# Attention, routed attention and a gated MLP on one core: the product with V on 128 partitions throughout, and a new issue order

## The chip, the cores and the metric

One core of a Trainium2 chip runs the whole program. The metric is the device time of one execution in microseconds (us); the median of several is given. The core has TensorE (PE: matmuls and transposes; PEld its weight loads), VectorE (DVE), ScalarE (ACT), GpSimd (POOL) and SyncE (SP, which here issues DMAs). Each engine works through its own queue in order; semaphores make one wait for another.

## What is computed

Three stages, each taking the output of the one before, over batch 8, sequence 576:

```python
# 1: attention, 8 heads of 64, block-causal in blocks of 64 (q, k, v: 8 x 8 x 576 x 64)
scores = where(block_i >= block_j, q @ k.T / 8, -1e9)
x = softmax(scores) @ v                      # heads side by side: 8 x 576 x 512
# 2: four routed attention experts of 64, causal, each token keeps its best 2 of 4
w = softmax over the top 2 of (x @ w_gate)
out = sum over e of w[e] * (softmax(causal(x wq[e] (x wk[e]).T / 8)) @ (x wv[e]) @ wo[e])
# 3: gated MLP with a product along the sequence
u, v = split(relu(out @ w_in)); v = layernorm(v)
y = (u * (w_spatial @ v + b_spatial)) @ w_out
```

Inputs and output are 32-bit; `w_in` and `w_out` arrive 64-bit.

## The kernel before

**Numbers in two halves.** Most operands are held as two 16-bit tiles, a rounded high part and the remainder (a cast, then a subtraction). A product is three matmuls, high x high, high x low, low x high, summed in PSUM.

**Pairs.** The heads are taken two at a time: four pairs of stage 1 and two pairs of experts per batch, 48 in all, keyed (batch, 0 to 3) and (batch, 4 to 5). A pair's sequence of 576 is five chunks: four of 128 and one of 64. For the last chunk the two heads' 64 queries share one block of 128. A pair goes through these steps:
- `load_qk`, `load_v` (lines 247 to 273): DMAs into a buffer `nat`, on SP, ACT or POOL. `mags` (line 275) finds the largest magnitudes, on DVE or ACT. `prep_qk` transposes q and k on PE and splits them (lines 343, 232, 238), `prep_v` splits v.
- `scores` (from line 371), four steps `sc` with j = 0 to 3 for four groups of query chunks: matmuls into a PSUM buffer `duo` (lines 389 to 407), row maxima on DVE (410, 412), the exponent's limit on ACT or DVE (420, 422), exponentials on ACT (426, 431). For j = 0 to 2 the matmuls contract over 64 partitions, one head in each half of the array; j = 3 uses 128.
- `weights` (line 437), steps `w`: the exponentials in 32 bits (`pf`, 1024, 1024, 512 and 576 columns for j = 0 to 3) are cast to 16 bits on ACT, DVE or POOL (lines 350, 352, 354) and the remainder is taken on DVE or POOL (line 448) into `p16`. `weights_t` (line 450) sends `p16` through a DMA transpose on SP (line 453) into `pT`, keys on the partitions.
- `av` (line 455), the product with V in three parts (24, 24 and 42 matmuls on PE, line 464). Chunk 4 runs over five key blocks; the fifth holds 64 keys, and its matmuls read partitions 0 to 63 only. One column of V is ones, so the row sums come along. Columns 1088 to 1151 and 2240 to 2303 of `p16`, behind the 64 keys, are cleared once at the start, and their rows of `pT` are zero.
- `halves` (line 488), step `x`: divides, casts, takes the remainder (line 498) and transposes by DMA into `x`.

There are four `duo` buffers (two PSUM banks each), four `nat`, four `pf`, three `p16`, four `pT`.

**Startup** converts and splits the weights once, among the first batches' steps: `split` is the split of wq/wk, wv and the gate (DVE part at line 238), `win`, `hl`, `wm`, `wout` make one matrix of wo and w_in.

**The dense part of a batch** (function `dense`): projections (line 804), values of the experts (827), the gate, the two expert pairs, then the first MLP product (883), the normalisation (`norm`, 921 to 927), the gated product along the sequence (`gating2`, 978 to 986, steps `gs`) and the last product (998) with its store.

**What sets the order.** All steps are generators, listed once with `add` (line 1294) and cut in pieces, one per engine visit. The tuple `ORDER` (line 1014) names for each next piece the number of its step: the whole program is issued by walking that tuple (line 1540), which fixes the order on each engine's queue and which buffer each step gets. `WAYS` (line 1198) says for each kind of step, with one letter or two per batch, on which engine it is issued: A, D, G or S for ACT, DVE, POOL or SP; "AG" in `w` is a cast on ACT and a subtraction on POOL. The last letter stands for all later batches. The planner that wrote the two tables is not in the kernel; the piece costs in `add` calls stay in the file but set nothing.

```python
for i in ORDER:
    t = named[i]
    ...
    run(t)
```

Of the kernel before, what the change touches and what calls it, by code (L numbers as in the profile page):

```python
# [21 lines left out]
P = 128  # L22
# [10 lines left out]
def attn_moe_gmlp_kernel(  # L33
# [18 lines left out]
    B, H, S, D = q.shape  # L52
# [402 lines left out]
    def av(p, wt):  # L455
# [3 lines left out]
        def chunk(c, hh, col, nk, pT):  # L459
            o = 65 * c  # L460
            for kk in range(nk):
                r = P if kk < 4 else 64
                for i, (t, a, n) in enumerate(((0, 0, 65), (0, 66, 64), (1, 0, 65))):
                    T.matmul(ps[:, hh, o:o + n], pT[0:r, col(t, kk):col(t, kk) + P], p.v[0:r, hh, kk, a:a + n],  # L464
                             start=kk == 0 and i == 0, stop=kk == nk - 1 and i == 2)
# [299 lines left out]
    def dense(b, keep):  # L765
# [821 lines left out]
```

## Time and profile before

| | |
|---|---|
| device time, median of 3 runs | 1056.85 us (1054.46 to 1057.37) |
| the profiled execution | 1055.53 us, of which the span of its instructions is 1053.8 us |
| mean granted TensorE clock | 0.928 of full speed |
| busy in the span | PE 902.1, DVE 791.7, ACT 669.8, POOL 469.6 us |

A busy time is the time in which at least one instruction of the engine was running. Matmuls overlap one another in the array, so that PE's busy time holds pauses shorter than one matmul's own duration; what a run of matmuls costs is read from the start of its first to the start of what follows. An engine's wait is put down to what came last before it. The granted clock is the share of full speed that TensorE was given in a stretch.

### The profile page before, as it was taken

To read this page: it belongs to the slowest core of one execution; us is meant where nothing else is said; L and a number is where in the kernel's file an instruction comes from. 1 tells how busy PE (TensorE), PEld (TensorE's weight loads), DVE (VectorE), ACT (ScalarE), POOL (GpSimd) and SP (SyncE) were. 2 spreads that over 40 slices of the span, in tenths; PEclk is the share of its full clock that TensorE was granted. 3 is DMA by queue.
4 is the path that set the end of the run, shared out by engine and by line. 5 is a ranking of instruction groups with operands and counts; after the bars stand their busy time and mean duration, and the time that the engine had idled before them with its cause. 6 is when DMAs were issued, how large, how long until landed. Compare 5 with 4: busy or idle time off the path is not lost.

```text
span 1053.8 us, 25324 instructions
## 1 busy us (share of the span) xinstructions
PE 902.1 (86%) x10118; PEld 654.3 (62%) x10118; DVE 791.7 (75%) x1616; ACT 669.8 (64%) x1206; POOL 469.6 (45%) x394
## 2 busy tenths in 40 slices
PE   1576697578999889988998899999998999799988
PEld 1355575466676657666776667667765776577654
DVE  4898989879887878687866787768768786657351
ACT  1786767767666756686858667677676756537331
POOL 4287665566323506454524538443463244304210
PEclk9968798688999899998999999999999999899989
DMA  9879866699659865889758986898479546924501
GB/s 212 162 146 186 183 134 142 128 168 194 122 101 179 160 125 101 156 169 179 138 111 164 160 160 119 147 186 160 78 150 176 96 76 121 189 31 72 106 21 45
DMA packets 492390, 143.66 MB, mean 136 GB/s; under 512 B 479712, under 2 KB 485968, under 8 KB 492272
## 3 DMA queue, kind: packets, MB, share of 16 engines
q1 hardware_dynamic: 472928, 131.38, 66.2%
q0 software_dynamic: 2832, 6.73, 2.3%
q10 hardware_dynamic: 16512, 3.94, 1.9%
q8 instruction: 79, 1.29, 0.5%
q14 instruction: 39, 0.32, 0.1%
HBM read 38.19 MB, written 9.44 MB: 45 GB/s over the span
## 4 chain that ended last, share of the span: by engine, by line
PE 46%; DVE 10%; ACT 5%; issue 2%; DMA 1%; ACTq 0%; SPq 0%; POOL 0%; DVEq 0%; POOLq 0%
PE duo L978 9%; PE duo L464 8%; PE duo L998 8%; PE duo L804 5%; PE duo L883 4%; PE duo L962 3%; PE duo L389 3%; DVE st L410 3%; PE duo L827 2%; ACT pf L431 2%; PE duo L404 2%; PE duo L343 1%; DVE qk L238 1%; DVE p L448 1%; ACT vn L924 1%
## 5 line engine op out<-in xcount | busy, mean ns | idle before, releaser
L448 POOL TENSOR_TENSOR p<-pf,p 128x1024 f16<-128x1024 f32 (+2 forms) x111 | 201.1, 1818 | 172.8 <-ACT p L350 74.4
L464 PEld LDWEIGHTS <-pT 128*128 128x128 f16 (+1 forms) x4320 | 159.6, 102 | 44.6 <-issue 23.4
L410 DVE TENSOR_REDUCE st<-duo 128x2 f32<-128x1024 f32 (+2 forms) x192 | 150.3, 816 | 36.4 <-PE duo L399 22.3
L389 PE MATMUL duo<-qk 64*128 64x256 f16 (+3 forms) x1152 | 118.5, 323 | 26.5 <-ACT qk L232 11.3
L464 PE MATMUL duo<-v,pT 128*128 128x65 f16 (+3 forms) x2880 | 117.0, 200 | 16.7 <-ACT pf L431 10.6
L978 PE MATMUL duo<-wsp,vn 128*128 128x288 f16 x896 | 122.9, 291 | 8.0 <-ACT vn L924 3.6
L431 ACT ACTIVATE pf<-duo,st,es 128x512 f32<-128x512 f32 (+3 forms) x224 | 122.0, 617 | 10.4 <-DVE rr L485 3.7
L998 PE MATMUL duo<-wo,gT 128*128 128x512 f16 (+1 forms) x480 | 109.2, 384 | 2.9 <-ACT pf L431 1.9
L498 POOL TENSOR_TENSOR xh<-pf,xh 128x640 f16<-128x640 f32 x40 | 57.6, 1439 | 121.4 <-ACT xh L350 115.5
L978 PEld LDWEIGHTS <-vn 128*128 128x128 f16 x896 | 87.0, 99 | 33.8 <-ACT vn L924 4.4
L804 PE MATMUL duo<-x,wqk 128*128 128x288 f16 x768 | 98.3, 287 | 0.6 <-DVE qk L238 0.5
L448 DVE TENSOR_TENSOR p<-pf,p 128x576 f16<-128x576 f32 (+2 forms) x81 | 83.3, 1034 | 15.2 <-ACT p L350 9.2
L389 PEld LDWEIGHTS <-qk 64*128 64x128 f16 x1152 | 52.3, 99 | 60.6 <-issue 35.9
L804 PEld LDWEIGHTS <-wqk 128*128 128x128 f16 x768 | 74.3, 98 | 21.5 <-issue 1.5
L350 ACT CAST p<-pf 128x1024 f16<-128x1024 f32 (+2 forms) x104 | 82.6, 809 | 1.2 <-DMA pT<-p 0.2
L998 PEld LDWEIGHTS <-gT 128*128 128x128 f16 (+1 forms) x480 | 47.3, 101 | 56.8 <-issue 5.3
L354 POOL TENSOR_SCALAR p<-pf 128x1024 f16<-128x1024 f32 (+2 forms) x46 | 42.7, 928 | 88.8 <-ACT pf L431 47.8
L343 PE MATMUL duo<-ident,nat 128*128 128x128 f32 x320 | 58.4, 319 | 18.3 <-ACT pf L431 6.1
L420 ACT ACTIVATE st<-st,ln,es 128x2 f32<-128x2 f32 (+2 forms) x91 | 35.0, 388 | 61.5 <-DVE st L410 44.3
L431 ACT ACTIVATE pf<-duo,st,mt 128x256 f32<-128x256 f32 (+3 forms) x128 | 69.9, 616 | 5.7 <-DVE st L422 4.3
L404 PE MATMUL duo<-qk 128*128 128x288 f16 x288 | 50.5, 318 | 20.1 <-ACT pf L431 15.2
L295 DVE TENSOR_REDUCE mst<-nat 128x1 f32<-128x640 f32 (+1 forms) x54 | 60.7, 1133 | 8.9 <-DMA nat<-in_v_dram 5.8
(269 smaller groups left out, 1742.7 us busy)
## 6 DMA issues: line engine op xcount, KB each, us to landing
out_dram<-o SPq DMA_DIRECT2D x16, 512.0 KB, 3.4
nat<-in_q_dram SPq DMA_DIRECT2D x52, 128.0 KB, 2.9
nat<-in_k_dram SPq DMA_DIRECT2D x52, 128.0 KB, 2.9
nat<-in_v_dram SPq DMA_DIRECT2D x40, 128.0 KB, 2.8
wf<-in_moe_w_in_dram SPq DMA_DIRECT2D x8, 512.0 KB, 4.8
nat<-in_v_dram POOLq DMA_DIRECT2D x20, 128.0 KB, 4.1
pT<-p SPq DMA_TRANSPOSE x144, 4.8
wf<-in_moe_w_out_dram SPq DMA_DIRECT2D x4, 512.0 KB, 4.9
```

The lines of the kernel that those rows point to most:

```text
L295: V.tensor_reduce(st[:, a, o], t[:, a].rearrange("p i c d -> p i (c d)"), op=OP.max, axis=AX.X, apply_absolute_value=True)
L343: T.transpose(ps[:, P * c:P * c + r], p.nat[0:r, i, c, :], ident[0:r, 0:r])
L350: A.copy(hi, src)
L389: T.matmul(ph[:, hh, o:o + w], p.q[hs, a, ts], p.k[hs, bb, 0:w], start=i == 0, stop=False)
L404: T.matmul(ps[:, MID + a:MID + a + n], p.q[:, l, 512:640], p.k[:, r, a:a + n], start=i == 0, stop=i == 2 and not (p.moe and a))
L410: V.reduce_max(st[:, 0, 2 * c:2 * c + 2], ph[:, :, off[c]:off[c] + P * (c + 1)], axis=AX.X)
L431: A.activation(pf[:, n * hh + off[c]:n * hh + off[c] + w], ph[:, hh, off[c]:off[c] + w], AF.Exp, bias=st[:, 1, 2 * c + hh:2 * c + hh + 1], ...
L448: (V if way[1] == "D" else G).tensor_sub(lo, src, hi)
L464: T.matmul(ps[:, hh, o:o + n], pT[0:r, col(t, kk):col(t, kk) + P], p.v[0:r, hh, kk, a:a + n], start=kk == 0 and i == 0, stop=kk == nk - 1 ...
L804: T.matmul(ps[:, MID + a:MID + a + w], wqk16[:, l, c, 2 * n + i, :], x16[c][:, r, a:a + w], start=m == 0, stop=m == 11)
L978: T.matmul(ps[:, MID + a:MID + a + n], vn[:, l, ds_], wsp16[:, r, c, a:a + n], start=i == 0, stop=False)
L998: T.matmul(ps[0:r, i], gT[:, x, d, P * c:P * c + r], wo16[:, y, d, :], start=m == 0, stop=m == 11)
```

## The change

In the product with V the fifth key block is read over all 128 partitions instead of 64. The matmuls are as many as before:

```diff
         def chunk(c, hh, col, nk, pT):
             o = 65 * c
             for kk in range(nk):
-                r = P if kk < 4 else 64
                 for i, (t, a, n) in enumerate(((0, 0, 65), (0, 66, 64), (1, 0, 65))):
-                    T.matmul(ps[:, hh, o:o + n], pT[0:r, col(t, kk):col(t, kk) + P], p.v[0:r, hh, kk, a:a + n],
+                    T.matmul(ps[:, hh, o:o + n], pT[:, col(t, kk):col(t, kk) + P], p.v[:, hh, kk, a:a + n],
                              start=kk == 0 and i == 0, stop=kk == nk - 1 and i == 2)
```

The two tables are new. `ORDER` has the same 3800 entries in another sequence (62 and 63 load the first pair, 66 and 67 the second, 70 and 71 the third; 1, 2 and 17 load weights; 158 and 159 make the first pair's scales, 78 and 79 its transposes):

```diff
     ORDER = (
-        0, 62, 62, 62, 62, 62, 62, 62, 1, 1, 1, 1, 1, 1, 1, 1, 66, 1, 67, 1, 67, 1, 67, 1, 64, 1, 66, 63, 66, 66,
-        158, 63, 66, 158, 63, 158, 66, 159, 17, 66, 159, 2, 159, 70, 159, 2, 70, 159, 3, 2, 70, 2, 70, 2, 70, 70, 2,
...
+        0, 62, 62, 62, 62, 62, 62, 62, 1, 1, 1, 1, 1, 1, 66, 1, 67, 1, 67, 1, 67, 1, 64, 66, 1, 63, 66, 1, 66, 158,
+        63, 1, 66, 158, 63, 158, 66, 159, 17, 66, 159, 2, 159, 70, 71, 71, 71, 159, 2, 159, 159, 78, 70, 79, 78, 2,
...
```

`WAYS` differs in 215 of its steps' entries. Two kinds of `w` as an example (first dense pair of each batch, j = 0 and 1), and the magnitudes of the first pair:

```diff
     WAYS = {
...
-        "w.4.0": ("AG", "AD", "GG", "AG", "AG", "AG", "DD", "AG"),
+        "w.4.0": ("AG", "AG", "DD", "GG", "AD", "AG", "AD", "DD"),
...
-        "w.4.1": ("DG", "GD", "GD", "GD", "DG", "GG", "GG", "DG"),
+        "w.4.1": ("DD", "DD", "GD", "DD", "DD", "GG", "AD", "DD"),
...
-        "mg.0.1": ("D",), "mg.1.0": ("D", "D", "D", "A", "D"), "mg.1.1": ("D", "D", "D", "A", "D", "A", "D"),
+        "mg.0.0": ("D", "D", "D", "A", "D", "A", "A", "D"), "mg.0.1": ("D", "D", "D", "A", "A", "A", "D", "A"),
```

Counted over all steps, before and after (number on each engine):

| kind | ACT | DVE | POOL | SP |
|---|---|---|---|---|
| casts of `w` and `x` | 144, 123 | 44, 61 | 52, 56 | |
| subtractions of `w` and `x` | | 89, 105 | 151, 135 | |
| limits of `sc` | 151, 132 | 41, 60 | | |
| magnitudes `mg` | 10, 20 | 54, 44 | | |
| split of v `pv` | 22, 21 | 5, 5 | 5, 6 | |
| `norm`, first operation | | 12, 16 | 28, 24 | |
| `norm`, last operation | | 12, 14 | 28, 26 | |
| remainder of `gs` | | 26, 20 | 6, 12 | |
| loads `lq` (7 DMAs each) | 3, 5 | | 3, 4 | 26, 23 |
| loads `lv` (3 DMAs each) | 2, 3 | | 10, 7 | 20, 22 |

Of the subtractions of 1024 columns, DVE has 30 before and 39 after, POOL 66 and 57.

## Rows read from the trace of the kernel before

**Rows 1.** The page: its first line and part 1 (busy us, share of the span, instructions).
```profile
span 1053.8 us, 25324 instructions
PE 902.1 (86%) x10118; PEld 654.3 (62%) x10118; DVE 791.7 (75%) x1616; ACT 669.8 (64%) x1206; POOL 469.6 (45%) x394
```

**Rows 2.** Stretches: us, PE, PEld, DVE, ACT, POOL busy (instructions), PEclk, DMA share, GB/s.
```profile
0.00:52.00 52.00, 20.30 (x118) 12.66 (x118) 34.93 (x100) 21.33 (x43) 16.78 (x41) 1.00 0.90 189
52.00:263.00 211.00, 151.75 (x1759) 118.12 (x1760) 185.84 (x326) 152.41 (x270) 140.45 (x108) 0.78 0.81 160
263.00:790.00 527.00, 490.97 (x5772) 358.69 (x5770) 406.17 (x829) 360.19 (x656) 239.08 (x194) 0.97 0.76 143
790.00:1053.80 263.80, 239.04 (x2473) 164.84 (x2471) 164.75 (x363) 135.87 (x239) 73.30 (x53) 0.95 0.49 94
```

**Rows 3.** Stretches of line 464's matmuls alone: us, PE busy (instructions), PEclk, DMA share, GB/s.
```profile
0.00:263.00 263.00, 40.46 (x900) 0.82 0.82 165
263.00:1053.80 790.80, 134.31 (x3420) 0.96 0.67 127
```

**Rows 4.** Timeline of PE, two stretches: start us, us, engine, line, operation, count.
```profile
546.63 1.63 PE L464 MATMUL duo<-v,pT 128*128 128x65 f16 x48
548.10 1.24 PE L998 MATMUL duo<-wo,gT 128*128 128x512 f16 x5
...
467.44 0.35 PE L389 MATMUL duo<-qk 64*128 64x128 f16 x6
467.61 0.21 PE L399 MATMUL duo<-m_col,m_row 64*128 64x64 bf16 x2
467.75 1.76 PE L464 MATMUL duo<-v,pT 128*128 128x65 f16 x42
469.44 0.86 PE L343 MATMUL duo<-ident,nat 128*128 128x128 f32 x5
```

**Rows 5.** Stretches of 0.1 us, line 464's matmuls alone (columns as in rows 3).
```profile
390.70:390.80 0.10, 0.10 (x10) 1.00 0.00 0
391.00:391.10 0.10, 0.10 (x5) 1.00 0.53 115
```

**Rows 6.** Line 464 on PE, 390.95 to 390.97 us: count, ns min/median/max, starts, forms.
```profile
L464 PE MATMUL duo<-v,pT x4: 191/192/201, 390.8 to 391.0; 128*128 128x65 f16 x2, 128*128 128x64 f16 x1, 64*128 64x65 f16 x1
```

**Rows 7.** The chain that ended last: start us, us, what.
```profile
608.98 3.05 PE duo L804 x24
```

**Rows 8.** Groups by line and shape: count, busy us, mean ns, idle before, releasers.
```profile
L448 POOL TENSOR_TENSOR p<-pf,p 128x1024 f16<-128x1024 f32 x66 | 145.2, 2202 | 129.3 <-ACT p L350 37.8 <-DVE p L352 35.7 <-issue 31.7
L448 DVE TENSOR_TENSOR p<-pf,p 128x1024 f16<-128x1024 f32 x30 | 37.5, 1254 | 2.1 <-POOL p L354 1.9
L448 DVE TENSOR_TENSOR p<-pf,p 128x512 f16<-128x512 f32 x14 | 10.3, 733 | 0.6 <-POOL p L354 0.2 <-ACT p L350 0.2
L352 DVE CAST p<-pf 128x576 f16<-128x576 f32 x4 | 3.8, 940 | 0.0
L352 DVE CAST p<-pf 128x512 f16<-128x512 f32 x5 | 2.9, 579 | 0.3 <-issue 0.3
L295 DVE TENSOR_REDUCE mst<-nat 128x2 f32<-128x1280 f32 x26 | 38.5, 1480 | 3.1 <-DMA nat<-in_k_dram 2.2 <-issue 0.6
L295 DVE TENSOR_REDUCE mst<-nat 128x1 f32<-128x640 f32 x28 | 22.6, 810 | 5.8 <-DMA nat<-in_v_dram 5.8
```

**Rows 9.** Waits of the sync queue (SP): line, waited for, us in total, times, longest.
```profile
SPq L453 <- POOL p L448: 114.3, 32, 33.0
```

**Rows 10.** Tile nat, loads issued from ACT: count, ns min/median/max, starts.
```profile
L255 ACTq DMA_DIRECT2D nat<-in_q_dram x6: 374/412/586, 134.9 to 433.6; - x6
```

**Rows 11.** Timeline of DVE and of PE before the first product with V.
```profile
64.07 2.34 DVE L238 SCALAR_TENSOR_TENSOR wqk<-x,sc,wqk 128x2048 f16<-128x2048 f32 x1
...
67.94 5.16 PE L464 MATMUL duo<-v,pT 128*128 128x65 f16 x90 [5.93 <-ACT pf L431]
```

**Rows 12.** Line 352, casts on DVE: count, ns min/median/max, starts, forms.
```profile
L352 DVE CAST p<-pf x42: 403/686/2617, 51.0 to 978.5; 128x1024 f16<-128x1024 f32 x33, 128x512 f16<-128x512 f32 x5, 128x576 f16<-128x576 f32 x4
```

463 rows, old and new, of tables (ORDER, WAYS) are left out of this document.

## The prediction

> **What bounds the kernel now.** Read the page first. The span is 1053.8 us; TensorE (PE) is busy for 902 us of it and VectorE (DVE) for 792 us [rows 1]. These shares are averages over unlike stretches, so the second view cuts the span in four [rows 2]. In the first 52 us PE is busy for 20 us: the loads and the first scales set the pace. From 52 to 263 us PE is busy for 152 of 211 us at a granted clock of 0.78, while DVE is busy for 186: here PE waits for what DVE, ScalarE (ACT) and GpSimd (POOL) hand it. From 263 us on PE is busy for 730 of 790.8 us (491.0 and 239.0), DVE for 571. There PE bounds: what PE no longer does there comes off the end nearly one for one, and DVE still has a quarter of the time free. The third view counts the product with V (line 464): 900 of its 4320 matmuls, ten of 48 whole products, lie in the first 263 us, the other 38 behind [rows 3].
>
> The fourth view shows what such a product costs. A run of 48 matmuls that all use 128 partitions starts at 546.63 and hands over at 548.10: 1.47 us, 30.6 ns each. A run of 42, the third part of a product with its six 64-partition matmuls in two groups of three, starts at 467.75 and hands over at 469.44: 1.69 us [rows 4]. At 30.6 ns it would take 1.29; 0.40 us is over. Slices of 0.1 us show where it sits: ten matmuls in flight in a plain slice, five in one where PE goes over to the 64-partition group [rows 5], and the forms in such a moment are those of line 464 with 64 rows [rows 6]. Going 128 to 64, back, to 64 again and back to the next 128-row work is four changes: **0.10 us each**.
>
> **The change, part by part.** (1) *Six matmuls with 128 rows in place of 64.* No matmul or weight load is added: 90 of each in a product, as before. The added rows of the key block are zeros in pT (the columns of p16 behind them are cleared once, and nothing writes there), and the tiles they come from are written over all partitions by the same transposes and splits, so no wait is added. What goes is the changes of row count. If a product is followed by 128-row work, four go. If it is followed by 64-row scores (line 389), the change into the scores was made early and three were paid, of which one stays: two go. Walking the issue order of before, 28 products are followed by 128-row PE work and 20 by scores: 28 x 4 + 20 x 2 = 152 changes. The new order has 38 and 10; walked over all PE pieces (scores of key groups 0 to 2 are 64-row, a k transpose ends with a 64-row block, the rest counts as 128) it has 256 changes where the old has 416. So 160 x 0.10 = 16.0 us of PE time. I take 38/48 of it, 12.7 us, in full, since it lies where PE bounds. Of the other 3.3 us I take 1.4: there PE is idle for a quarter of the time, and a shorter product mostly ends in a longer wait. Sum: 14.1 us. The ends: 12.7 if nothing early counts; 18 if all counts and the early ones, at a mean clock of 0.82 [rows 3], cost more than 0.10.
>
> A rule speaks against this part. In this trace, six score matmuls of 128 columns start within 0.17 us (467.44 to 467.61), 28 ns each [rows 4], while a 288-column, 128-row matmul takes 3.05 us / 24 = 127 ns, 0.44 ns a column [rows 7], which would be 56 ns for 128 columns: 64-row matmuls on different partition halves do run two at a time. The Trainium skill, page TensorEngine Tiling (Array Packing), section When to Use Tiling, advises 2x row tiling where the contraction is 64 or less; by it the 64-row form should be kept. If each of the six went at half a plain 30.6 ns, the change would give back 48 x 6 x 15 ns = 4.4 us and the sum would be 9.7, not 14.1. But all six read partitions 0 to 63 and stand in threes, so no second half is there to run beside them, and the 42-run is longer, not shorter, than 42 plain ones: I keep 14.1.
>
> (2) *The engine of each copy.* Counted over the table of ways, with 215 of its entries changed: subtractions on DVE go from 89 to 105 and on POOL from 151 to 135; casts on DVE from 44 to 61, on ACT from 144 to 123, on POOL from 52 to 56. DVE takes 9 more subtractions of 1024 at 1.254 us and 7 more of 512 at 0.733 (those of 576 and 640, 4 fewer and 4 more, nearly cancel): +16 us. Of its 17 more casts, 4 of 576 at 0.94, 6 of 512 at 0.579, 8 of 640 taken at 0.579 too, and one of 1024 fewer: +11. The other kinds (ten fewer magnitude scans, eight at 0.81 and two at 1.48, and six fewer remainders of the gate against 19 more row limits and six more norm steps) come to some -4. DVE +23 us, POOL about -20 (nine fewer 1024 subtractions at 2.202 alone are -19.8) [rows 8]. On DVE this adds 23 to 792. By batch, summing the same entries: +4 in batches 0 and 1, +22 in 2 to 5, -6 in 6, +3 in 7. In the stretch 263 to 790 it makes DVE some 430 of 527 us, still under PE's 491 less 9. Cost taken: none, PE covers it; if that cover is gone, the upper end is all 23 us. The lower end is a gain: POOL subtractions feed the transposes, and the sync queue's longest wait is for them, 114 us [rows 9]; shorter waits there may give back some of PE's 61 idle us behind 263. I take 0, the row nearest being the busy times of the late stretch.
>
> (3) *Loads.* Three q/k loads of seven DMAs and seven v loads of three change queue: SP has 15 fewer DMAs, ACT 17 more, POOL 2 fewer. On ACT each holds the queue for some half a microsecond (412 ns in the median for one kind) [rows 10]: 7 to 8 us over the run, on a queue that loses 21 casts and 19 row limits for ten magnitude scans. Their data are asked for tens of microseconds ahead; cost 0, at worst 8.
>
> (4) *The order.* 624 PE pieces stand in nearly the same order, the median one moved by two places. The clearest move is at the start: before the first product (67.94 us) DVE ran the three weight splits, 2.34 us the longest [rows 11]; the new order puts them behind it, with 73 DVE pieces ahead of it in place of 80. But ahead of batch 0's fourth product stand 121 in place of 122, and ahead of its last 283 in place of 278: what is won first is owed again by then. The tail, after the last product, keeps its work. Cost 0, between -18 (startup carried through and some late idle time filled) and +20 (as much lost).
>
> **Sum.** The profiled execution took 1055.53 us (span 1053.8), 1.3 below the median 1056.85 of three runs. 1055.5 - 14.1 = 1041.4; put against the median 1042.8. I say **1042**.
>
> **The rivals.** *The new plan also fills idle time* (chance 0.24). For it: 59 us of PE idle from 52 to 263, 61 after; costs taken from traces fit the chip better. Against: the same count of DVE pieces ahead of batch 0's later products. A sixth of that idle time, 16 us, on top: 1026.
>
> *DVE becomes the bound* (0.15), the slower side. Place: batches 2 to 5, where most of the added copies sit. Each has to come between a PE result and the transposes that the next product needs, and a DVE cast can be held up: 0.69 us in the median, 2.62 at worst [rows 12]. The Trainium skill, SBUF — State Buffer, section Who interferes with whom, says a DVE instruction with two SBUF inputs, as these subtractions have, or in a 2-port mode, and a POOL instruction block each other for the whole instruction. If all of DVE's 23 us reach the end, 1042 + 23 = 1065. It decides once more than 14 us of them do; against it stand PE's 93% and DVE's 77% in that stretch.
>
> *The shorter product only makes PE wait sooner* (0.09): every 0.4 us saved goes into the next wait for a transpose or a free PSUM buffer. For it: 61 us of late idle time. Against: most of it lies in pieces of a few us, not behind each product. Time: 1055, no change. That 64-row groups persist in another place can't be: the edit takes the row count away.
>
> **How the numbers follow.** Forecast case 0.52, which ends faster. A measurement of this kernel tells 0.3%, 3 us, from none. Faster: 0.52 + 0.24 = 0.76; same 0.09; slower 0.15. Low end: the filled-idle case with the whole 18 of the order in it and a little more of the early changes, 1020. High end: half-way into the DVE case and past no change, 1060. The forecast case alone spans 1035 to 1048.
>
> **What would show it.** Line 464 should have one form with 128 rows, its 42-runs should take 1.3 us, and PE's busy time should fall by 10 to 16 us. DVE should be near 815 us busy, POOL near 450. Behind 263 us PE should stay at 92% or more; if it falls to 90% with waits for DVE in front of transposes, the DVE rival is right. I am wrong in mechanism if 42-runs stay at 1.7 us.

## The result, and the profile after

The changed kernel takes **1065.76 us** (median of four runs, 1063.49 to 1067.48). Four runs of the kernel before on the same chip gave 1055.8. The ratio is 1.0093, with a 95% interval from 1.0066 to 1.0119: slower by 0.9%, where 1042 was forecast and the range ended at 1060.

The changed kernel's page, its first line and part 1 (columns as in [rows 1]; lines behind 462 have a number one lower now, so that the product with V is line 463):

```profile
span 1065.8 us, 25305 instructions
PE 893.7 (84%) x10118; PEld 647.0 (61%) x10118; DVE 805.7 (76%) x1658; ACT 659.8 (62%) x1189; POOL 449.4 (42%) x381
```

PE is busy for 8.4 us less than before, yet the span is 12.0 longer: PE's idle time, span less busy, went from 151.7 to 172.1 us, and these 20.4 us less the 8.4 are the 12.0. Where PE idles, the four stretches of the changed kernel say (columns as in [rows 2]):

```profile
0.00:52.00 52.00, 15.78 (x81) 10.07 (x82) 31.82 (x96) 15.41 (x29) 19.06 (x41) 0.88 0.84 177
52.00:263.00 211.00, 145.28 (x1615) 114.44 (x1615) 173.29 (x302) 137.70 (x242) 129.50 (x101) 0.72 0.75 147
263.00:790.00 527.00, 482.90 (x5752) 351.20 (x5745) 423.34 (x874) 363.20 (x668) 218.25 (x172) 0.96 0.78 143
790.00:1065.80 275.80, 249.73 (x2679) 171.29 (x2678) 177.23 (x390) 143.47 (x252) 82.62 (x68) 0.97 0.56 102
```

In the first 263 us PE gets 1696 matmuls done, where the kernel before had 1877 [rows 2]. From 52 to 263 every engine is less busy than before, DVE too (173 us against 186), and TensorE's granted clock is 0.72 against 0.78. No engine became the bound there: PE waits more, and part of what it does runs at a lower clock.

The product itself did what was asked. PE's timeline of the changed kernel (columns as in [rows 4]):

```profile
486.90 1.44 PE L463 MATMUL duo<-v,pT 128*128 128x65 f16 x42
488.18 2.62 PE L343 MATMUL duo<-ident,nat 128*128 128x128 f32 x20
...
505.21 1.45 PE L463 MATMUL duo<-V,pT 128*128 128x65 f16 x42
506.50 3.10 PE L803 MATMUL duo<-x,wqk 128*128 128x288 f16 x24
```

A run of 42 hands over after 1.28 and 1.29 us; it was 1.69 [rows 4].

### The profile page after: what moved, and what is told of

It is laid out like the page before. It is cut to its first block, busy times and chain, and to the rows that moved or that the text cites. A ratio compares the mean times of both kernels' runs of the same rounds, so it can differ in the third digit from the quotient of the medians.

```text
span 1065.8 us, 25305 instructions
## 1 busy us (share of the span) xinstructions
PE 893.7 (84%) x10118; PEld 647.0 (61%) x10118; DVE 805.7 (76%) x1658; ACT 659.8 (62%) x1189; POOL 449.4 (42%) x381
## 3 DMA queue, kind: packets, MB, share of 16 engines
q8 instruction: 79, 1.29, 0.5%
## 5 line engine op out<-in xcount | busy, mean ns | idle before, releaser
L448 POOL TENSOR_TENSOR p<-pf,p 128x1024 f16<-128x1024 f32 (+2 forms) x99 | 181.8, 1841 | 127.4 <-ACT p L350 74.0
L463 PEld LDWEIGHTS <-pT 128*128 128x128 f16 x4320 | 151.8, 102 | 53.6 <-DMA pT<-p 27.0
L463 PE MATMUL duo<-v,pT 128*128 128x65 f16 (+1 forms) x2880 | 106.7, 200 | 21.2 <-ACT pf L431 11.1
L448 DVE TENSOR_TENSOR p<-pf,p 128x1024 f16<-128x1024 f32 (+2 forms) x93 | 93.3, 1013 | 24.6 <-ACT p L350 17.2
L354 POOL TENSOR_SCALAR p<-pf 128x1024 f16<-128x1024 f32 (+2 forms) x50 | 48.3, 968 | 147.8 <-ACT pf L431 105.6
L389 PEld LDWEIGHTS <-qk 64*128 64x128 f16 x1152 | 47.6, 101 | 73.8 <-issue 44.8
L431 ACT ACTIVATE pf<-duo,st,mt 128x256 f32<-128x256 f32 (+3 forms) x128 | 70.0, 617 | 16.3 <-DVE st L422 10.9
L350 ACT CAST p<-pf 128x512 f16<-128x512 f32 (+2 forms) x91 | 72.6, 812 | 6.1 <-DMA pT<-p 5.3
L463 PE MATMUL duo<-V,pT 128*128 128x65 f16 (+1 forms) x1440 | 52.7, 197 | 20.2 <-DMA pT<-p 12.9
L343 PE MATMUL duo<-ident,nat 128*128 128x128 f32 (+1 forms) x320 | 54.4, 306 | 15.3 <-ACT pf L431 8.6
L826 PE MATMUL duo<-wvg,x 128*128 128x260 f16 x480 | 57.8, 279 | 1.7 <-DVE qk L816 1.6
```

The source lines that it names most:

```text
L343: T.transpose(ps[:, P * c:P * c + r], p.nat[0:r, i, c, :], ident[0:r, 0:r])
L350: A.copy(hi, src)
L389: T.matmul(ph[:, hh, o:o + w], p.q[hs, a, ts], p.k[hs, bb, 0:w], start=i == 0, stop=False)
L431: A.activation(pf[:, n * hh + off[c]:n * hh + off[c] + w], ph[:, hh, off[c]:off[c] + w], AF.Exp, bias=st[:, 1, 2 * c + hh:2 * c + hh + 1], ...
L448: (V if way[1] == "D" else G).tensor_sub(lo, src, hi)
L463: T.matmul(ps[:, hh, o:o + n], pT[:, col(t, kk):col(t, kk) + P], p.v[:, hh, kk, a:a + n], start=kk == 0 and i == 0, stop=kk == nk - 1 and ...
```

## The experiments

Each row is the median of one kernel's runs, and its ratio to runs of the kernel before on the same chip. "Old" and "new" are the tables of before and after the change. The runs of before vary by up to 2 us in the median from one group of rows to the next, so that a difference of two rows is good to that; where it matters the ratios are compared.

| kernel | product with V | tables | us | ratio [95%] |
|---|---|---|---|---|
| mm_only | 128 rows | old | 1047.0 | 0.9929 [0.9906, 0.9951] |
| tables_only | 64 rows | new | 1077.7 | 1.0221 [1.0184, 1.0259] |
| order_new | 128 | new order, old engines | 1079.6 | 1.0243 [1.0208, 1.0277] |
| ways_new | 128 | old order, new engines | 1081.0 | 1.0263 [1.0225, 1.0300] |
| early_new | 128 | new up to entry 1076, old behind | 1072.9 | 1.0157 [1.0130, 1.0184] |
| early_old | 128 | old up to entry 1084, new behind | **1043.1** | 0.9866 [0.9840, 0.9891] |
| head_new | 128 | new up to 408, old behind | 1054.1 | 0.9986 [0.9961, 1.0011] |
| cut_570 | 128 | new up to 570, old behind | 1066.1 | 1.0107 [1.0083, 1.0132] |
| cut_772 | 128 | new up to 772, old behind | 1070.8 | 1.0146 [1.0104, 1.0188] |
| mid_new | 128 | old to 408, new to 1076, old behind | 1074.4 | 1.0189 [1.0146, 1.0231] |
| loads_old | 128 | new, moved loads on their old queues | 1062.1 | 1.0061 [1.0041, 1.0081] |
| weights_back | 128 | new, MLP weight steps where the old order has them | 1088.4 | 1.0316 [1.0278, 1.0353] |
| weights_ahead | 128 | old, those steps where the new order has them | 1072.4 | 1.0168 [1.0146, 1.0189] |
| weights_loads_back | 128 | weights_back and loads_old together | 1082.2 | 1.0269 [1.0232, 1.0306] |
| after_av_later | 128 | new, early products up to 4 places later | 1083.9 | 1.0261 [1.0229, 1.0293] |
| after_av_later8 | 128 | new, early products up to 8 places later | 1086.9 | 1.0282 [1.0256, 1.0308] |
| mm_av_sooner | 128 | old, early products up to 4 places sooner | 1093.6 | 1.0343 [1.0311, 1.0374] |
| mm_av_later | 128 | old, early products up to 4 places later | 1060.3 | 1.0047 [1.0028, 1.0066] |

### The matmuls and the tables apart

`mm_only` has the edit of `chunk` alone; `tables_only` has both tables and the old `chunk`; `order_new` and `ways_new` have the new `chunk` with one table each.

```diff
# mm_only against the kernel before
-                r = P if kk < 4 else 64
...
# tables_only against the changed kernel
+                r = P if kk < 4 else 64
```

mm_only: 

> The 128-row matmuls alone, with the order and the engine table of the kernel before. Theory A (the matmuls give what the row-count changes cost, the new tables cost more than that): 28 x 4 + 20 x 2 = 152 changes x 0.10 us = 15.2 us less PE time, 12 to 14 us of it at the end: 1056 - 13 = 1043 us, ratio 0.988. Theory B (PE only waits sooner, the matmuls give nothing): 1054 to 1057, ratio 1.00. Either way the third part of a product takes 1.3 us in place of 1.7.

tables_only: 

> The new order and engine table, with the fifth key block still read over 64 partitions. Theory A: 428 changes of row count in place of 256 put back 172 x 0.10 = 17 us of PE time, some 14 at the end: 1066 + 14 = 1080 us, ratio 1.023. Theory B: 1066, ratio 1.009.

order_new: 

> 128-row matmuls, the new order, but the engine of every copy, limit and load as before. If the order is what costs (products held behind work they do not need): as the changed kernel or above, 1060 to 1075. If the 23 us more work on VectorE are what costs (the DVE rival): back to 1042 to 1048. An order made for other engines can also lose by the mismatch alone, so that both mixed kernels come out above 1066: then the two tables only work together, and the loss has to be looked for by stage.

ways_new: 

> 128-row matmuls, the order as before, but the engines of the new table. If the added 23 us on VectorE are what costs: 1060 to 1070. If the order costs: near the matmuls alone, 1042 to 1050. If the tables only work together: above 1066.

The matmuls alone win 0.7%, some 7.5 us (5.2 to 9.9 by the interval). The tables take that back and more: 1047.0 to 1065.8, **19 us** (17 by the ratios). With the new tables the matmuls are worth more: 1077.7 to 1065.8 is 12 us (13 by the ratios), so that the tables cost 23 us where the product keeps its 64 rows. The two ways round agree on the whole, some 10 us slower. With the new order and the old engines the loss against `mm_only` is 33 us, with the old order and the new engines 34, with both 19. Either table loses more without the one that it came with, so these two runs can't share the 19 us out between order and engines.

### Early and late

All steps up to one entry of `ORDER` follow one pair of tables, the rest the other; a step keeps the engine of the table under which it began. Entries 1076 to 1084 lie among the first heads of batch 2, while batch 1's experts are still to come; PE gets there at 356 us in early_old and at 380 us in the changed kernel.

```diff
# early_old (the others alike); the tuple is written out in the kernel
-    ORDER = NEW
+    ORDER = OLD[:1084] + [the entries of NEW that are not yet issued, in NEW's order]
```

early_new: 

> 128-row matmuls. The first 1076 of the 3800 entries of the new order, with the new engines for the steps that begin there (up to about the first product of batch 2, 260 to 300 us into the run), then the rest in the old order with the old engines. Against the matmuls alone (1047) and the changed kernel (1066). Theory E (the new tables lose in the early part, where all engines wait for one another): 1061 to 1067. Theory M (they lose in batches 2 to 5, where 22 of the 23 us more VectorE work lie): 1046 to 1052.

early_old: 

> 128-row matmuls. The reverse: the first 1084 entries of the old order with the old engines, then the rest in the new order with the new engines. Theory E: 1043 to 1051, near the matmuls alone, in spite of 22 us more work on VectorE. Theory M: 1060 to 1068.

PE's timeline, the first projections (line 803) of batches 0, 2, 3, 5 and 6, in the changed kernel (columns as in [rows 4], and in brackets the idle time ahead and what ended it):

```profile
153.09 3.10 PE L803 MATMUL duo<-x,wqk 128*128 128x288 f16 x24
...
382.08 3.10 PE L803 MATMUL duo<-x,wqk 128*128 128x288 f16 x24
...
506.50 3.10 PE L803 MATMUL duo<-x,wqk 128*128 128x288 f16 x24
...
723.17 1.26 PE L803 MATMUL duo<-x,wqk 128*128 128x288 f16 x9
...
836.34 3.10 PE L803 MATMUL duo<-x,wqk 128*128 128x288 f16 x24 [0.61 <-ACT pf L431]
```

The same in early_old, whose tables are the same from batch 2 on:

```profile
133.66 3.16 PE L803 MATMUL duo<-x,wqk 128*128 128x288 f16 x24
...
359.05 3.10 PE L803 MATMUL duo<-x,wqk 128*128 128x288 f16 x24
...
485.32 3.10 PE L803 MATMUL duo<-x,wqk 128*128 128x288 f16 x24
...
700.90 1.26 PE L803 MATMUL duo<-x,wqk 128*128 128x288 f16 x9
...
812.99 3.10 PE L803 MATMUL duo<-x,wqk 128*128 128x288 f16 x24 [0.62 <-ACT pf L431]
```

The changed kernel is 19.4 us behind in batch 0 (where the two orders differ in what stands ahead of this point), 23.0 in batch 2, 21.2 in batch 3, 22.3 in batch 5, 23.4 in batch 6. The spans end 24.3 apart. So nearly the whole loss is made in the first 380 us, and what is lost there is never caught up. The late part of the new tables is no burden: early_old is faster than mm_only (the intervals don't overlap), and at 0.9866 it beats both kernels. The two halves nearly add: early_new loses 26 us against mm_only (6 us more than the upper end of theory E), early_old wins 4, and both together lose 19.

At batch 2's projections both kernels have done the same 2983 matmuls, so that the 23.0 us can be divided. The changed kernel, then early_old (columns as in [rows 2]):

```profile
0.00:382.08 382.08, 267.61 (x2983) 201.83 (x2984) 296.44 (x583) 234.71 (x418) 192.54 (x174) 0.82 0.77 150
```

```profile
0.00:359.05 359.05, 256.67 (x2983) 192.42 (x2984) 291.69 (x577) 236.06 (x424) 191.87 (x176) 0.82 0.84 160
```

PE is idle for 114.5 us against 102.4, 12.1 more, and busy for 10.9 us more with the same matmuls. The longer busy time is the clock. TensorE's clock has two levels in these traces, 1.2 and 2.4 GHz (0.5 and 1.0 of full speed). Of PE's busy time 104 us lie at the lower level in the changed kernel and 80 in early_old; with a microsecond there counted as half of one at the upper level, the two come to 215.6 and 216.7. So about half of the lag is waiting, and half is matmuls that ran at the lower clock. This is one profiled execution each, but the other runs point the same way: the mean granted clock is 0.914 to 0.922 in the four of the changed kernel and 0.919 to 0.936 in the four of early_old. Whether the clock was lower because PE waited more, no run here separates. Of the added waiting, 6.6 us end with a transpose into pT, the largest part. PE's list of waits up to the same points (line, waited for, us in total, times, longest), changed kernel, then early_old:

```profile
PE duo L463 <- DMA pT<-p: 11.5, 7, 2.5
```

```profile
PE duo L463 <- DMA pT<-p: 4.9, 4, 1.9
```

head_new: 

> 128-row matmuls. Only the first 408 entries new (up to batch 0's fourth product, some 120 us), then old. By the times of the products, the changed kernel is 4 us behind the matmuls alone there: 1047 + 4 = 1051 if the loss by then is carried to the end and no more comes, 1047 if it is caught up; 1060 or more if the head sets the whole loss.

cut_570: 

> 128-row matmuls; the first 570 entries new (up to about batch 1's first product, 176 us in the changed kernel), the rest old. The changed kernel is 10 us behind the matmuls alone at that product, 4 of them by entry 408. Bit by bit: 1047 + 10 = 1057, within 3. One place behind it: 1051 to 1054, as with 408 entries. One place before it: 1065 or more.

cut_772: 

> 128-row matmuls; the first 772 entries new (up to batch 0's first product of the experts, 240 us), the rest old. The changed kernel is 15 us behind there. Bit by bit: 1047 + 15 = 1062, within 3. One place behind it: near the run with 570. One place before it: 1070 or more.

mid_new: 

> 128-row matmuls; the first 408 entries old, those up to 1076 new, the rest old. If head and middle add: 1073 (the run with 1076 new entries) less 7 for the head, 1066. If the middle loses only because the head was new (state left behind by it): near 1047, up to 1053.

Against mm_only's 1047.0 the loss grows with the place of the cut: 7 us with 408 new entries, 19 with 570, 24 with 772, 26 with 1076. The runs with 570 and 772 came out 9 us above what "bit by bit" gave and fall under "one place before it"; the largest step, 12 us, lies between entries 408 and 570. But `mid_new`, with the old startup up to entry 408 and the new entries behind, loses 27 us, so that the startup isn't needed for the loss, and head and middle don't add (7 and 27 against 26). These figures hold what the joint of two tables costs by itself, since the joints differ, and no run tells that cost apart. So no one place is shown to make the loss, and where it lies within the first 1076 entries stays open.

### Which steps

`loads_old` puts the ten loads that changed queue back; `weights_back` and `weights_ahead` move the steps that make the MLP's weights (`win` to `wf3`), which stand earlier among the other pieces in the new order (110 of their 114 entries, by 23 places in the median).

```diff
# loads_old: the letters of lq and lv in WAYS, all others new
-        "lq", "lv": the ten letters that the change altered
+        "lq", "lv": the letters of before
# weights_back: only the entries of these steps move in ORDER
```

loads_old: 

> The changed kernel with the ten q, k and v loads that moved between queues put back on the queues of before, nothing else. ScalarE then issues 40 DMAs in place of 57; in the changed kernel's trace it issues for 35 us in place of 20, and once, at 153 us, stands still for 4.4 us in front of such an issue until a transpose has landed. If these loads cost: 1066 - 6 to 1066 - 15, 1051 to 1060. If not: 1063 to 1068.

weights_back: 

> The changed kernel with one part of its order undone: the steps that convert and multiply w_in and w_out (win, hl, wm, wx, wout, wf1 to wf3) stand where the old order has them among the other pieces. The new order has them up to 57 pieces earlier, in a stretch in which every engine waits for others. Theory W (weights taken up too early hold back the pairs): 1066 - 5 to 1066 - 13, 1053 to 1061. Theory P (the order of the pairs' own steps loses): 1063 to 1069.

weights_ahead: 

> The reverse: 128-row matmuls with the old order and engines, and only these weight steps as early as the new order has them. Theory W: 1047 + 5 to 1047 + 13, 1052 to 1060. Theory P: 1045 to 1050.

weights_loads_back: 

> The changed kernel with both undone: the weight steps at their old places and the ten moved loads on their old queues. If the two add (the loads alone gave 4 us): 1049 to 1057 under theory W, 1060 to 1064 under theory P.

The loads cost some 4 us: 1062.1 against 1065.8, with intervals that overlap, and 6 us where the weight steps are back too (1082.2 against 1088.4). The weight steps can't be told guilty: put back, the kernel loses 23 us more; put ahead in the old order, it loses 25. A few other entries changed places with them (at least 6 and 9). These runs are inconclusive on the weight steps.

### The distance between scores and product

A count in the two orders showed a suspect. Between the last scores that a part of a product with V needs and the part itself lie, in the first twelve pairs, 18.4 us of PE work in the old order (median of 36 parts) and 14.6 in the new one. In that time the exponentials, casts, subtractions and DMA transposes must be done. PE's list of waits from 52 to 263 us (line, waited for, us in total, times, longest) in the changed kernel speaks for it:

```profile
PE duo L463 <- DMA pT<-p: 9.5, 6, 2.5
PE duo L389 <- ACT pf L426: 8.2, 3, 3.7
PE duo L389 <- ACT pf L431: 4.8, 3, 3.6
PE duo L210 <- DVE dgb L205: 4.7, 2, 4.0
```

The same row in mm_only and in the kernel before:

```profile
PE duo L463 <- DMA pT<-p: 4.0, 3, 2.0
```

```profile
PE duo L464 <- DMA pT<-p: 1.4, 2, 0.9
```

Four kernels move the early products:

```diff
# after_av_later; the kernels alike with 8 places, or in the old order, sooner or later
-    ORDER = NEW
+    ORDER = NEW with the three PE entries of each ("av", key) of the first twelve pairs up to 4 PE entries later
```

The buffers allow less than that for most parts. Counted against the other PE pieces, 10 of the 36 parts stand four or more places later in after_av_later and in after_av_later8 (there by up to eight) and 9 in mm_av_later, and the median part stands one place later; in mm_av_sooner 20 stand four places sooner. Between 44 and 54 entries of other steps moved along, by up to 23 places.

after_av_later: 

> The changed kernel; in the first twelve pairs each part of the product with V is issued four PE pieces later (as far as buffers allow), with what depends on it behind it. PE's work between the last scores a part needs and the part itself goes from 14.6 to 17.0 us in the median of these 36 parts; the kernel before has 18.4. Theory 'the products stand too close behind their scores': 8 to 20 us of the lost 19 come back, 1046 to 1058. Rival 'the new order loses by what its other steps wait for': nothing comes back or more is lost, 1063 to 1085.

after_av_later8: 

> As the other, eight pieces later: the median distance becomes 18.1 us of PE work, six of 36 parts under 15 (nine in the kernel before, nineteen in the changed one). Theory 'too close': at least as much comes back as with four, 1046 to 1056. Rival: 1063 or more.

mm_av_sooner: 

> 128-row matmuls with the old tables; in the first twelve pairs each part of the product with V is issued four PE pieces sooner: median distance 18.4 to 15.2 us, as in the new order. Theory 'too close': loses 8 to 20 us against 1047, so 1055 to 1067, with PE's waits for the transposes before 263 us growing from 4 us to about 10. Rival: within 3 us of 1047.

mm_av_later: 

> The same kernel with each of these parts four pieces later than in the old order: median distance 19.9 us. A control: theory 'too close' says 1042 to 1050 (little is left to win); 'any shift of a few places in this plan loses' says 1055 or more here and in all three others.

The remedy fails: with the distance widened, the changed kernel doesn't win 8 to 20 us but loses 18 and 21 more. The same row of waits:

In after_av_later (52 to 263 us):

```profile
PE duo L463 <- DMA pT<-p: 11.0, 3, 4.3
```

In mm_av_sooner (52 to 263 us):

```profile
PE duo L463 <- DMA pT<-p: 27.4, 7, 8.6
```

Up to four places sooner in the old order, PE stands 27.4 us for transposes and the kernel loses 47 us, so the distance does matter. But widened in the changed kernel these waits stay (11.0 us against 9.5), so that the two runs don't tell what the kernel would take without them. In the old order, where mm_av_later has no such wait left, the move later cost 13 us. So the distance as it was moved here gives nothing back, and the theory is neither shown nor shut out for the 6.6 us above. All four runs agree with the other sentence of the control: any shift of a few places among the early steps loses.

## Why the prediction was wrong

**What bounds the kernel**: right. PE bounds behind 263 us, and the lag made ahead of 380 us stays to the end within some 3 us.

**Term (1), the changes of row count**: right in its mechanism, too large in its size. The run of 42 takes 1.28 to 1.29 us, the 1.29 that was worked out. mm_only's page, its first line and part 1:

```profile
span 1044.1 us, 25324 instructions
PE 889.2 (85%) x10118; PEld 645.1 (62%) x10118; DVE 787.5 (75%) x1616; ACT 670.2 (64%) x1206; POOL 472.3 (45%) x394
```

PE's busy time there is 12.9 us less than in [rows 1]; 152 changes at 0.10 us are 15.2. With a busy microsecond at the lower clock counted as half, the 128-row matmuls save 19.4 us with the old tables (844.0 to 824.6) and 15.4 with the new (840.4 to 825.0), so that PE's work fell by about what was forecast. The time fell by 7.5 us (5.2 to 9.9) with the old tables and by 12 to 13 with the new, where 14.1 were in the sum. What was sized too high is "I take 38/48 of it, 12.7 us, in full, since it lies where PE bounds". In the pair of profiled executions 19.4 us became 9.7: 3.2 went into longer idle time, and 6.5 into busy time at the lower clock, for which the sum had no term (the kernel before is at a mean of 0.928 there, mm_only at 0.915; other runs of before go down to 0.914, so that this split is of these two executions alone). The rival "the shorter product only makes PE wait sooner" was right for the first part. The remark on 64-row matmuls that run two at a time came out as it was weighed: the Trainium skill, page TensorEngine Tiling (Array Packing), section When to Use Tiling, would have kept the 64-row form, and the trace speaks for the 128-row form where only one half is in use and the work around it has 128 rows. The same page of the Trainium skill, section Key Properties, says that a change of tiling mode drains TensorE; 0.40 us less for four changes fewer agrees with that.

**Term (2), the engines**: POOL came as forecast, 449.4 us (near 450 was said); DVE rose by 14 us to 805.7, where 23 were worked out (near 815). The cost of none holds for the late batches: early_old carries DVE at

```profile
PE 882.0 (85%) x10118; PEld 637.0 (61%) x10118; DVE 801.3 (77%) x1652; ACT 660.4 (63%) x1193; POOL 448.4 (43%) x383
```

(its page, part 1) and is the fastest of all. This settles the **DVE rival**: its number, 1065, is the measured one, but by luck, since its place was batches 2 to 5, and hardly anything is lost there. PE's late share, 732.6 of 802.8 us or 91%, lay between the two signs that the prediction gave and told nothing by itself. Groups by line and shape in the changed kernel (columns as in [rows 8]):

```profile
L448 POOL TENSOR_TENSOR p<-pf,p 128x1024 f16<-128x1024 f32 x57 | 126.9, 2228 | 85.5 <-ACT p L350 42.3 <-DVE p L352 19.5 <-DVE rr L484 9.9
L448 DVE TENSOR_TENSOR p<-pf,p 128x1024 f16<-128x1024 f32 x39 | 51.2, 1315 | 13.3 <-ACT p L350 9.5 <-POOL p L354 3.6
```

The nine subtractions moved as counted; one of DVE's takes 61 ns longer than in [rows 8]. The gain that was held possible here, shorter waits of the sync queue for POOL, did not come: that wait is 126.3 us in the changed kernel, 114.3 before [rows 9].

**Term (3), the loads**: 0 was taken, at worst 8; some 4 were measured, not far outside the noise.

**Term (4), the order**: this is the step that failed: "Cost 0, between -18 … and +20". The new tables cost 17 to 19 us with the 128-row product and 23 with the 64-row one, at the upper end of that range or past it; the value taken was 0, and the total range did not reach there, since it left this upper end out and took only half of DVE's. Two readings led to it. "624 PE pieces stand in nearly the same order, the median one moved by two places" was taken for a proof that little changes. But the early stretch is sensitive to such moves: in the four kernels above, moves of up to four places (eight in one), one place in the median of three of them, cost 13 to 47 us. And it looked at PE alone, whose pieces moved by 22 places at most, while the 1239 pieces that DVE has in the table of before moved by four in the median and by up to 79. Then "the same count of DVE pieces" ahead of batch 0's later products says how many they are, not when each can run: PE's waits in that stretch are for ACT, DVE, POOL and the transposes alike. Nor had the sum a term for the clock, which made about half of the lag at batch 2. The first product does start sooner, as predicted, at

```profile
63.86 4.40 PE L463 MATMUL duo<-v,pT 128*128 128x65 f16 x90 [0.25 <-ACT pf L431]
```

(PE's timeline of the changed kernel) against 67.94 [rows 11]; at the end of batch 0's fourth product, at 127 us in mm_only, the changed kernel is 4 us behind it, at the end of the first expert pair's, at 226 us, it is 15.

**What stays open** is why the early part of the new tables runs slower. Shown is that the loss is made ahead of batch 2's projections, that there it is about half waiting and half matmuls at the lower clock (against early_old), that the engines of the copies are not its cause late in the run, and that the moved loads are about a fifth of it. Over the whole run, PE's work with the lower clock counted as half is the same in the changed kernel and in mm_only (825.0 and 824.6 us); of the 21.7 us between their profiled spans 17.2 are idle time and 4.5 the clock, since mm_only has more of its late batches at the lower level (45 us busy there behind batch 2's projections, against 33). Not shown is which steps of the early order make PE wait, and whether the lower clock follows from the waits. That the new plan's own account of costs was off in the startup, where loads, conversions and the first pairs compete, would fit, and was not tried.

## What to carry to other kernels

Price a new issue order from its densest stretch: where every engine waits for another, moves of up to four places cost 13 to 47 us here, none of the four tried gained, and 0 is not the middle of what an unknown order can cost. Split a change that has a local edit and a new plan into its halves, and a plan into early and late, before explaining it: one cut in time gave a kernel 2.1% faster than the one that was handed over. Where one engine bounds the rest of the run, compare two kernels by when a landmark of each batch starts; a lag that stays constant tells where it was made. Where both have done the same matmuls at a landmark, split the lag into idle time and busy time, and the busy time by the clock's level.

## What the runs showed of the hardware

A DMA issue on ACT's queue can hold ACT for a transfer of another queue. ACT's timeline in the changed kernel (with the queue's DMA issues; in brackets the idle time and what ended it):

```profile
151.78 0.48 ACTq L259 DMA_DIRECT2D nat<-in_q_dram  x1
152.31 0.59 ACT L729 COPY wo<-duo 128x512 f32<-128x512 f32 x1 [0.43 <-PE duo L726]
157.28 0.48 ACTq L259 DMA_DIRECT2D nat<-in_q_dram  x1
157.81 0.39 ACT L420 ACTIVATE st<-st,ln,es 128x1 f32<-128x1 f32 x1 [4.91 <-DMA pT<-p]
```

ACT stood from 152.9 to 157.3 us ahead of issuing a load of q, until a transpose issued by SP had landed. SP's queue shows it (columns as above):

```profile
151.50 1.35 SPq L453 DMA_TRANSPOSE pT<-p  x1
```

It landed at 157.20, and the issue of the load waits for the very semaphore on which this transpose counts; loads and transposes share semaphores in this program. In loads_old the same stall is there (4.6 us), and neither the kernel before nor mm_only has one for a transpose longer than 0.2 us, though the load stands on ACT in them too. In order_new, with the new order and the old engines, it is there too (4.8 us). So this stall comes with the new order, which decides what is under way when the load is issued.
